# A pointwise convolution on TensorE: head and tail chunks side by side in one buffer, and a last supertile in two column parts

## The chip, the cores and the metric

One core of a Trainium2 chip. The metric is the device time of one execution in microseconds. The profiler's span is about 1.7 us shorter than the device time of the same execution (576.7 for 578.42 before the change).

## The reference, cut to what matters

```python
# x: (1, 384, 384, 384) bf16, dw: (1, 1, 384), pw: (384, 384)
out = x * dw[0, 0]                    # depthwise part with k = 1: a scale per channel
return einsum('bhwc,cd->bhwd', out, pw)
```

So it is one matrix product: 147,456 rows of 384 channels times a 384 x 384 matrix, whose rows are scaled by dw once at the start. 113 MB are read and 113 MB are written.

## The kernel before

The rows are cut into 288 supertiles of 512. VectorE transposes 32 x 32 blocks of a supertile's input (two instructions), TensorE makes 48 matmuls of 384 columns into four PSUM banks, ScalarE evicts the four banks (copies them out to SBUF) as bf16. Two PSUM sets alternate. Loads and stores move chunks of 1 to 10 supertiles, each chunk in the next of three input and three output buffers (an excerpt; comments are added):

```python
head, tail = [1, 1, 2, 2, 3, 4, 5], [7, 5, 4, 2, 1, 1]       # chunk sizes; 10 between
Xs = [bufp.tile([P, 4 * LMAX, C], BF16, name=f"X{i}") for i in range(NX)]      # NX = 3
Os = [bufp.tile([P, 4 * LMAX * D], BF16, name=f"O{i}") for i in range(NO)]     # NO = 3
...
with nc.tensor.Fori(0, NS // 2, 1) as it:                     # NS = 288
    rv = nc.tensor.to_reg(it + 1)
    for s in range(2):
        supertile(s, rv)                                      # 48 matmuls
...
for jj, (t, j) in enumerate(order):                           # evictions
    if j == 0 and t >= NO:
        nc.scalar.wait_ge(s_o[t % NO], 16 * (t // NO))        # store of chunk t - 3 has landed
    nq = 4
    if jj + 1 == NS:                                          # the last: VectorE takes half
        nq = 2
        ...
        e = nc.vector.tensor_copy(Ov[:, nq:4, j, :], PS[s][:, nq:4, :D])
    a = nc.scalar.copy(Ov[:, 0:nq, j, :], PS[s][:, 0:nq, :D])
```

The last supertile leaves in two stores, one issued by ScalarE (ACT in the profile) and one by the sync engine (SP), each of two 768-byte rows a partition.

## Time and profile before

| | before |
|---|---|
| device time, median of 3 (range) | 578.25 us (578.11 to 578.52) |
| span of the profiled execution | 576.7 us |
| TensorE busy | 98% |
| loop of matmuls, first to last | 7.40 to 571.22 us |
| TensorE's one pause | 19.31 to 21.11 us |
| last store issued, landed | 572.23, 575.3 us |

The lines behind these rows are in the prediction below.

### The profile page before, as it was taken

To read this page: it belongs to the slowest core of one execution; us is meant where nothing else is said; L and a number is where in the kernel's file an instruction comes from. 1 tells how busy PE (TensorE), PEld (TensorE's weight loads), DVE (VectorE), ACT (ScalarE), POOL (GpSimd) and SP (SyncE) were. 2 spreads that over 40 slices of the span, in tenths; PEclk is the share of its full clock that TensorE was granted. 3 is DMA by queue.
4 is the path that set the end of the run, shared out by engine and by line. 5 is a ranking of instruction groups with operands and counts; after the bars stand their busy time and mean duration, and the time that the engine had idled before them with its cause. 6 is when DMAs were issued, how large, how long until landed. Compare 5 with 4: busy or idle time off the path is not lost.

```text
span 576.7 us, 29717 instructions
## 1 busy us (share of the span) xinstructions
PE 567.1 (98%) x13871; PEld 356.0 (62%) x13871; DVE 508.8 (88%) x582; ACT 419.0 (73%) x296; POOL 1.7 (0%) x8
## 2 busy tenths in 40 slices
PE   8899999999999999999999999999999999999996
PEld 5566666666666666666666666666666666666663
DVE  6789999999999999999999999999999999999994
ACT  6677777777777777777777777777777777777774
POOL 1000000000000000000000000000000000000000
PEclk9999999999999999999999999999999999999999
DMA  7999999999999999999999999999999999986987
GB/s 243 388 432 436 422 424 425 432 439 421 407 388 438 386 392 395 430 398 384 404 421 400 394 405 425 387 386 427 405 386 394 427 407 389 400 356 272 365 342 266
DMA packets 25964, 226.88 MB, mean 393 GB/s; under 512 B 1249, under 2 KB 5218, under 8 KB 21986
## 3 DMA queue, kind: packets, MB, share of 16 engines
q1 hardware_dynamic: 25680, 226.60, 97.8%
q10 hardware_dynamic: 274, 0.20, 0.1%
q14 instruction: 9, 0.07, 0.0%
q8 instruction: 1, 0.02, 0.0%
HBM read 113.54 MB, written 113.25 MB: 393 GB/s over the span
## 4 chain that ended last, share of the span: by engine, by line
PE 96%; DMA 1%; ACT 1%; issue 0%; DVE 0%; POOL 0%; POOLq 0%; ACTq 0%; SPq 0%
PE ps L153 96%; DMA out_dram<-O 1%; ACT O L287 1%; PE ps L172 0%; ACT w_r L259 0%; DVE O L284 0%; PE ps L203 0%; POOL zero L220 0%; POOL warm L219 0%; POOLq L320 0%; PE ps L187 0%; ACTq L279 0%; SPq L93 0%
## 5 line engine op out<-in xcount | busy, mean ns | idle before, releaser
L153 PE MATMUL ps<-w_r,T 32*128 32x384 bf16 x13824 | 562.0, 321 | 2.7 <-ACT O L287 1.8
L246 DVE STREAM_TRANSPOSE T<-X 128x384 uint32<-128x384 uint32 x576 | 505.9, 881 | 56.4 <-DMA X<-in_x_dram 3.7
L287 ACT CAST O<-ps 128x1536 bf16<-128x1536 f32 x288 | 413.8, 1437 | 149.9 <-PE ps L153 147.1
L153 PEld LDWEIGHTS ps<-w_r,T 32*128 32x128 bf16 x13824 | 353.8, 93 | 210.8 <-ACT O L287 2.2
L259 ACT CAST w_r<-ps 128x768 bf16<-128x768 f32 x5 | 3.6, 818 | 1.6 <-PE ps L203 1.6
L172 PE MATMUL ps<-zero 32*128 32x384 bf16 x32 | 2.8, 516 | 1.4 <-POOL zero L220 1.4
L284 DVE CAST O<-ps 128x768 bf16<-128x768 f32 x1 | 1.0, 958 | 3.0 <-PE ps L153 3.0
L264 DVE COPY dw_f<-ps 128x3 f32<-128x3 f32 x1 | 0.2, 161 | 3.0 <-PE ps L187 3.0
L203 PE MATMUL ps<-pw_n,sel_w 128*128 128x384 bf16 x12 | 2.4, 329 | 0.0
L232 ACT ACT_TABLE_LOAD x1 | 1.3, 1283 | 1.5 <-SPq L93 1.5
L172 PEld LDWEIGHTS ps<-zero 32*128 32x128 bf16 x32 | 1.1, 118 | 2.0 <-issue 1.7
L203 PEld LDWEIGHTS ps<-pw_n,sel_w 128*128 128x128 bf16 x12 | 1.0, 99 | 1.7 <-DMA pw_n<-in_pw_dram 0.6
L259 DVE CAST w_r<-ps 128x768 bf16<-128x768 f32 x1 | 1.0, 958 | 0.9 <-PE ps L203 0.9
L268 DVE TENSOR_SCALAR sel_w<-sel,dw_f 128x512 bf16<-128x512 bf16 x3 | 0.9, 348 | 0.1
L222 POOL TENSOR_SCALAR_AFFINE_SELECT sel<-ones 128x512 bf16<-128x512 bf16 x1 | 0.7, 737 | 0.1
L221 POOL MEMSET ones<- 128x512 bf16 x1 | 0.5, 531 | 0.0
L187 PEld LDWEIGHTS ps<-ones,dw_row 1*128 1x128 bf16 x3 | 0.3, 127 | 0.3 <-issue 0.2
L232 ACT COPY warm<-warm 128x1 f32<-128x1 f32 x2 | 0.3, 188 | 0.0
L220 POOL MEMSET zero<- 128x192 uint32 x1 | 0.3, 258 | 0.0
L187 PE MATMUL ps<-ones,dw_row 1*128 1x1 bf16 x3 | 0.3, 174 | 0.0
L219 POOL MEMSET warm<- 128x3 f32 x1 | 0.1, 101 | 0.5 <-SPq L93 0.5
L309 POOL MEMSET const-bfloat16-1.0<- 128x1 bf16 x1 | 0.1, 102 | 0.0
(3 smaller groups left out, 0.3 us busy)
## 6 DMA issues: line engine op xcount, KB each, us to landing
X<-in_x_dram SPq DMA_DIRECT2D x25, 3840.0 KB, 21.9
out_dram<-O SPq DMA_DIRECT2D x25, 3840.0 KB, 27.9
X<-in_x_dram SPq DMA_DIRECT2D x2, 1920.0 KB, 14.6
out_dram<-O SPq DMA_DIRECT2D x2, 1920.0 KB, 16.8
X<-in_x_dram SPq DMA_DIRECT2D x2, 1536.0 KB, 10.4
out_dram<-O SPq DMA_DIRECT2D x2, 1536.0 KB, 13.5
X<-in_x_dram SPq DMA_DIRECT2D x1, 2688.0 KB, 20.1
out_dram<-O SPq DMA_DIRECT2D x1, 2688.0 KB, 12.0
```

The costliest lines, as they stand in the source:

```text
L153: mm = nc.tensor.matmul(PS[s][:, q, :D], lhsT=Ts[s][32 * q : 32 * q + 32, b, par::2], rhs=w_r[32 * q : 32 * q + 32, b, par, :], start=(b = ...
L172: nc.tensor.matmul(PS[0][:, i % 4, :D], lhsT=zero[32 * (i % 4) : 32 * (i % 4) + 32, 0:P], rhs=zero[32 * (i % 4) : 32 * (i % 4) + 32, :], s ...
L187: mm = nc.tensor.matmul(PS[1][:, k, D : D + 1], lhsT=dw_row[:, P * k : P * k + P], rhs=ones[0:1, 0, 0:1], start=True, stop=True,)
L203: mm = nc.tensor.matmul(w_ps(b)[:, r, :], lhsT=sel_w[:, b // 2, 2 * (b % 2) + r, :], rhs=pw_n[:, b // 2, :], start=True, stop=True,)
L221: nc.gpsimd.memset(ones[:], 1.0).then_inc(s_seed)
L222: nc.gpsimd.affine_select(out=sel[:].rearrange("p (v r) (q w) -> p v r q w", v=2, q=4), in_=ones[:].rearrange("p (v r) (q w) -> p v r q w" ...
L232: c = nc.scalar.copy(warm[:, s + 1 : s + 2], warm[:, 0:1])
L246: ins = nc.vector.transpose(out=Tw[:, 3 * h : 3 * h + 3], in_=Xw[:, :, j, 96 * h : 96 * h + 96].rearrange("p k (b w) -> p b k w", w=32),)
L259: i = nc.vector.tensor_copy(out, in_) if e == 0 else nc.scalar.copy(out, in_)
L268: nc.vector.tensor_scalar_mul(sel_w[:, k], sel[:], dw_f[:, k : k + 1]).then_inc(s_sw)
L284: e = nc.vector.tensor_copy(Ov[:, nq:4, j, :], PS[s][:, nq:4, :D])
L287: a = nc.scalar.copy(Ov[:, 0:nq, j, :], PS[s][:, 0:nq, :D])
```

## The change

Its intent is to take away the pause and to shorten the end. Chunks become groups: the small chunks of the head share one buffer, and so do those of the tail, so that none waits for another's store. At the end, the last supertile is computed in two column parts, so that what is evicted after the last matmul is smaller; for that the last four supertiles leave the loop. A new order of rows in the last load makes the last store one run of 3072 bytes a partition. The diff is an excerpt, with lines joined and comments added.

```diff
-    head, tail = [1, 1, 2, 2, 3, 4, 5], [7, 5, 4, 2, 1, 1]
+    head, tail = [[1, 1, 2, 2, 4]], [[6, 4], [3, 2, 1, 1, 1]]     # groups: one buffer each
...
-            if t >= NX: d._wait_ge(s_t[je % 2][1], je // 2 + 1)
+            if i == 0 and g >= NR:                                 # only a group's first chunk waits
+                nc.sync.wait_ge(s_t[je % 2][1], je // 2 + 1)
...
+            # last load:  xf[512 * first :, :].rearrange("(a k q) c -> q a k c", k=4, q=4)
+            # last store: of[512 * first :, :].rearrange("(m q) d -> m (q d)", q=4)
...
-        with nc.tensor.Fori(0, NS // 2, 1) as it:
+        with nc.tensor.Fori(0, NS // 2 - 2, 1) as it:
...
+        supertile(0, NS // 2 - 1)
+        supertile(1, NS // 2 - 1)
+        supertile(0, NS // 2)
+        for ps, c0, c1 in ((1, 0, DS), (0, DS, D)):                # DS = 256
+            ...                                                    # 48 matmuls of c1 - c0 columns
...
+                parts = [(s, 0, D, 2, 2 * jj + 2)]                 # supertile 286: both engines
+                parts = [(1, 0, DS, 2, 2 * jj + 1), (0, DS, D, 2, 2 * jj + 2)]   # the last
```

More of the change, by code (lines that the diff above doesn't have):

```diff
@@ L13, with _groups @@
 LMAX = 10
-NX = 3
-NO = 3
-def _chunks(n_super: int):
-    head, tail = [1, 1, 2, 2, 3, 4, 5], [7, 5, 4, 2, 1, 1]
-    mid = n_super - sum(head) - sum(tail)
+NR = 3
+DS = 256
+def _groups(n_super: int):
+    head, tail = [[1, 1, 2, 2, 4]], [[6, 4], [3, 2, 1, 1, 1]]
+    mid = n_super - sum(map(sum, head + tail))
     assert mid > 0 and mid % LMAX == 0
-    return head + [LMAX] * (mid // LMAX) + tail
+    return head + [[LMAX]] * (mid // LMAX) + tail
 @with_exitstack
@@ L51 @@
     NS = N // 512
-    chunks = _chunks(NS)
+    groups = _groups(NS)
+    chunks, first = [], 0
+    for g, ls in enumerate(groups):
+        for i, L in enumerate(ls):
+            chunks.append((g, i, sum(ls[:i]), first, L))
+            first += L
     NT = len(chunks)
-    s0 = [sum(chunks[:t]) for t in range(NT)]
+    g_end = [max(c[3] + c[4] for c in chunks if c[0] == g) - 1 for g in range(len(groups))]
     consts = ctx.enter_context(tc.tile_pool(name="consts", bufs=1))
@@ L68 @@
     zero = consts.tile([P, D], BF16, name="zero")
-    Xs = [bufp.tile([P, 4 * LMAX, C], BF16, name=f"X{i}") for i in range(NX)]
+    Xs = [bufp.tile([P, 4 * LMAX, C], BF16, name=f"X{i}") for i in range(NR)]
     Ts = [bufp.tile([P, NB, 256], BF16, name=f"T{i}") for i in range(2)]
-    Os = [bufp.tile([P, 4 * LMAX * D], BF16, name=f"O{i}") for i in range(NO)]
+    Os = [bufp.tile([P, 4 * LMAX * D], BF16, name=f"O{i}") for i in range(NR)]
     PS = [psum.tile([P, 4, 512], F32, name=f"ps{s}") for s in range(2)]
-    s_x = [nc.alloc_semaphore(f"s_x{i}") for i in range(NX)]
+    s_x = [[nc.alloc_semaphore(f"s_x{i}{k}") for k in range(max(map(len, groups[i::NR])))] for i in range(NR)]
     s_t = [[nc.alloc_semaphore(f"s_t{i}{h}") for h in range(2)] for i in range(2)]
@@ L79 @@
     s_d = nc.alloc_semaphore("s_d")
-    s_o = [nc.alloc_semaphore(f"s_o{i}") for i in range(NO)]
+    s_o = [nc.alloc_semaphore(f"s_o{i}") for i in range(NR)]
     s_dw = nc.alloc_semaphore("s_dw")
@@ L90 @@
     s_zero = nc.alloc_semaphore("s_zero")
-    s_last = nc.alloc_semaphore("s_last")
     with tc.tile_critical():
         def load_x(t):
-            L = chunks[t]
-            r = 512 * s0[t]
-            src = xf[r : r + 512 * L, :].rearrange("(p s) c -> p (s c)", p=P)
-            d = nc.sync.dma_start(Xs[t % NX][:, : 4 * L, :].rearrange("p s c -> p (s c)"), src)
-            if t >= NX:
-                je = s0[t - NX] + chunks[t - NX] - 1
-                d._wait_ge(s_t[je % 2][1], je // 2 + 1)
-            d.then_inc(s_x[t % NX], 16)
-        def store(t):
-            L = chunks[t]
-            r = 512 * s0[t]
-            je = s0[t] + L - 1
-            dst = of[r : r + 512 * L, :].rearrange("(q p j) d -> p q (j d)", q=4, p=P)
-            src = Os[t % NO][:, : 4 * L * D].rearrange("p (q e) -> p q e", q=4)
-            nc.sync.wait_ge(s_a[je % 2], je // 2 + 2)
-            nc.sync.dma_start(dst, src).then_inc(s_o[t % NO], 16)
+            g, i, off, first, L = chunks[t]
@@ new lines, in load_x @@
+            dst = Xs[g % NR][:, 4 * off : 4 * (off + L), :]
+            if t + 1 < NT:
+                src = xf[512 * first : 512 * (first + L), :].rearrange("(p s) c -> p (s c)", p=P)
+                dst = dst.rearrange("p s c -> p (s c)")
+            else:
+                src = xf[512 * first :, :].rearrange("(a k q) c -> q a k c", k=4, q=4)
+            if i == 0 and g >= NR:
+                je = g_end[g - NR]
+                nc.sync.wait_ge(s_t[je % 2][1], je // 2 + 1)
+            nc.sync.dma_start(dst, src).then_inc(s_x[g % NR][i], 16)
@@ new lines, in store @@
+        def store(t):
+            g, i, off, first, L = chunks[t]
+            je = first + L - 1
+            src = Os[g % NR][:, 4 * off * D : 4 * (off + L) * D]
+            if t + 1 < NT:
+                dst = of[512 * first : 512 * (first + L), :].rearrange("(q p j) d -> p q (j d)", q=4, p=P)
+                src = src.rearrange("p (q e) -> p q e", q=4)
+                nc.sync.wait_ge(s_a[je % 2], je // 2 + 2)
+                if je >= NS - 2:
+                    nc.sync.wait_ge(s_d, 1)
+            else:
+                dst = of[512 * first :, :].rearrange("(m q) d -> m (q d)", q=4)
+                nc.sync.wait_ge(s_a[1], NS // 2 + 2)
+                nc.sync.wait_ge(s_d, 3)
+            nc.sync.dma_start(dst, src).then_inc(s_o[g % NR], 16)
@@ L114 @@
         nc.scalar.dma_start(dw_row[:], dw.rearrange("a e c -> a (e c)")).then_inc(s_dw, 16)
         nc.sync.dma_start(pw_n[:], pw.rearrange("(k p) d -> p k d", p=P)).then_inc(s_pw, 16)
-        for t in range(NX + 1):
-            load_x(t)
-        for t in range(NT - 1):
-            for u in (t + NX, t + NX + 1):
-                if NX < u < NT and (u == t + NX) != (chunks[u - NX] == 1 and u - NX < 4):
-                    load_x(u)
-            store(t)
-        o_last = Os[(NT - 1) % NO][:, : 4 * D].rearrange("p (q e) -> p q e", q=4)
@@ L125 @@
-        of_last = of[N - 512 :, :].rearrange("(q p) d -> p q d", p=P)
-        nc.sync.dma_start(of_last[:, 2:4], o_last[:, 2:4])._wait_ge(s_d, 1).then_inc(
-            s_last, 16
-        )
-        for o in range(NO):
-            nc.sync.wait_ge(s_o[o], 16 * len(range(o, NT - 1, NO)))
-        nc.sync.wait_ge(s_last, 32)
+        todo = []
+        for t, (g, i, off, first, L) in enumerate(chunks):
+            todo.append((g_end[g - NR] if g >= NR else -1, load_x, t))
+            todo.append((first + L + 1, store, t))
@@ L137 @@
+        for _, f, t in sorted(todo, key=lambda a: a[0]):
+            f(t)
+        for o in range(NR):
+            nc.sync.wait_ge(s_o[o], 16 * sum(map(len, groups[o::NR])))
         w_eng = [1, 0, 1, 1, 1, 1]
@@ L216 @@
                 supertile(s, rv)
+        supertile(0, NS // 2 - 1)
+        supertile(1, NS // 2 - 1)
+        supertile(0, NS // 2)
+        for ps, c0, c1 in ((1, 0, DS), (0, DS, D)):
+            for b in range(NB):
+                for par in range(2):
+                    for q in range(4):
+                        if par == 0 and q == 0:
+                            if ps == 1 and b in (0, 3):
+                                nc.tensor.wait_ge(s_t[1][b // 3], NS // 2)
+                            if b == 0:
+                                nc.tensor.wait_ge(s_a[ps], NS // 2 + (ps == 0))
+                                if ps == 0:
+                                    nc.tensor.wait_ge(s_d, 1)
+                        mm = nc.tensor.matmul(
+                            PS[ps][:, q, : c1 - c0],
+                            lhsT=Ts[1][32 * q : 32 * q + 32, b, par::2],
+                            rhs=w_r[32 * q : 32 * q + 32, b, par, c0:c1],
+                            start=(b == 0 and par == 0),
+                            stop=(b == NB - 1 and par == 1),
+                            tile_position=(32 * q, 0),
+                        )
+            mm.then_inc(s_pe)
         nc.gpsimd.memset(warm[:], 0.0).then_inc(s_seed)
@@ L237, in transposes @@
         def transposes(t, j):
-            jj = s0[t] + j
-            L = chunks[t]
+            g, i, off, first, L = chunks[t]
+            jj = first + j
             s = jj % 2
-            Xw = Xs[t % NX][:].bitcast(U32)[:, : 4 * L, :].rearrange("p (k l) c -> p k l c", l=L)
+            Xw = Xs[g % NR][:].bitcast(U32)[:, 4 * off : 4 * (off + L), :].rearrange("p (k l) c -> p k l c", l=L)
             Tw = Ts[s][:].bitcast(U32).rearrange("p b (i k) -> p b k i", k=4)
@@ L244, in transposes @@
                 if h == 0 and j == 0:
-                    nc.vector.wait_ge(s_x[t % NX], 16 * (t // NX + 1))
+                    nc.vector.wait_ge(s_x[g % NR][i], 16 * sum(len(ls) > i for ls in groups[g % NR : g + 1 : NR]))
                 ins = nc.vector.transpose(
@@ L252, in transposes @@
                 ins.then_inc(s_t[s][h])
-        order = [(t, j) for t in range(NT) for j in range(chunks[t])]
+        order = [(t, j) for t in range(NT) for j in range(chunks[t][4])]
         def w_out(b):
@@ L274 @@
         for jj, (t, j) in enumerate(order):
-            L = chunks[t]
+            g, i, off, first, L = chunks[t]
             s = jj % 2
-            Ov = Os[t % NO][:, : 4 * L * D].rearrange("p (q j d) -> p q j d", q=4, d=D)
-            if j == 0 and t >= NO:
-                nc.scalar.wait_ge(s_o[t % NO], 16 * (t // NO))
-            nq = 4
-            if jj + 1 == NS:
-                nq = 2
-                nc.vector.wait_ge(s_o[t % NO], 16 * (t // NO))
-                e = nc.vector.tensor_copy(Ov[:, nq:4, j, :], PS[s][:, nq:4, :D])
-                e._wait_ge(s_pe, 2 * jj + 2)
-                e.then_inc(s_d)
-            a = nc.scalar.copy(Ov[:, 0:nq, j, :], PS[s][:, 0:nq, :D])
-            a._wait_ge(s_pe, 2 * jj + 2)
-            a.then_inc(s_a[s])
+            Ov = Os[g % NR][:, 4 * off * D : 4 * (off + L) * D].rearrange("p (q j d) -> p q j d", q=4, d=D)
+            if j == 0 and i == 0 and g >= NR:
+                nc.scalar.wait_ge(s_o[g % NR], 16 * sum(map(len, groups[g % NR : g : NR])))
+            if jj + 2 < NS:
+                parts = [(s, 0, D, 4, 2 * jj + 2)]
+            elif jj + 2 == NS:
+                nc.vector.wait_ge(s_o[g % NR], 16 * sum(map(len, groups[g % NR : g : NR])))
+                parts = [(s, 0, D, 2, 2 * jj + 2)]
+            else:
+                parts = [(1, 0, DS, 2, 2 * jj + 1), (0, DS, D, 2, 2 * jj + 2)]
+            for ps, c0, c1, nq, v in parts:
+                if nq < 4:
+                    e = nc.vector.tensor_copy(Ov[:, nq:4, j, c0:c1], PS[ps][:, nq:4, : c1 - c0])
+                    e._wait_ge(s_pe, v)
+                    e.then_inc(s_d)
+                a = nc.scalar.copy(Ov[:, 0:nq, j, c0:c1], PS[ps][:, 0:nq, : c1 - c0])
+                a._wait_ge(s_pe, v)
+                a.then_inc(s_a[s])
             if jj + 2 < NS:
                 transposes(*order[jj + 2])
-        nc.scalar.dma_start(of_last[:, 0:2], o_last[:, 0:2])._wait_ge(s_a[(NS - 1) % 2], (NS - 1) // 2 + 2).then_inc(
-            s_last, 16
-        )
 _INS = ['x', 'dw', 'pw']
```

## The prediction

> **What bounds the kernel now.** I read the busy table first, then the chain of waits, then the head and the tail in order of time. A "supertile" below is 512 rows of x: 48 matmuls into four PSUM banks, one eviction, two vector transposes.
>
> ```profile
> PE 567.1 (98%) x13871; PEld 356.0 (62%) x13871; DVE 508.8 (88%) x582; ACT 419.0 (73%) x296; POOL 1.7 (0%) x8
> ...
> L153 PE MATMUL ps<-w_r,T 32*128 32x384 bf16 x13824 | 562.0, 321 | 2.7 <-ACT O L287 1.8
> L246 DVE STREAM_TRANSPOSE T<-X 128x384 uint32<-128x384 uint32 x576 | 505.9, 881 | 56.4 <-DMA X<-in_x_dram 3.7
> L287 ACT CAST O<-ps 128x1536 bf16<-128x1536 f32 x288 | 413.8, 1437 | 149.9 <-PE ps L153 147.1
> ```
>
> TensorE works 98% of the span, so only its edges can move: before its first matmul, its one pause, and after its last. The chain in order of time shows all three.
>
> ```profile
> 7.40 2.16 PE ps L153 x48
> 9.56 0.02 issue
> 9.58 1.45 ACT O L287
> 11.03 0.02 issue
> 11.05 8.49 DMA out_dram<-O
> 19.54 0.02 issue
> 19.56 0.02 ACTq L279
> 19.57 0.04 issue
> 19.62 1.45 ACT O L287
> 21.07 0.05 issue
> 21.11 550.11 PE ps L153 x13536
> 571.22 0.02 issue
> 571.25 0.96 DVE O L284
> ```
>
> Matmuls begin at 7.40. The first supertile takes 2.16 us; from 21.11 on, 282 supertiles take 550.11 us without a break, 1.951 us each. The pause lies between: supertiles 1 to 5 end at 9.56 + 5 x 1.951 = 19.31, the next starts at 21.11, so TensorE loses 1.80 us. The chain names the reason: the fourth chunk wants output buffer 0 again, and the first chunk's store, issued at 11.05, lands only 8.49 us later. ScalarE then evicts late, and the matmuls wait for their banks. The stretch view confirms that the pause is whole, and shows the tail.
>
> ```profile
> 19.30:21.10 1.80, 0.00 (x0) 0.00 (x0) 1.80 (x4) 1.48 (x2) 0.00 (x0) 1.00 0.94 378
> ...
> 571.30:572.20 0.90, 0.00 (x0) 0.00 (x0) 0.90 (x1) 0.74 (x1) 0.00 (x0) 1.00 1.04 348
> 572.20:574.20 2.00, 0.00 (x0) 0.00 (x0) 0.00 (x1) 0.00 (x0) 0.00 (x0) 1.00 1.02 317
> ```
> ```profile
> 571.24 0.80 ACT L287 CAST O<-ps 128x768 bf16<-128x768 f32 x1 [0.51 <-PE ps L153]
> 571.25 0.96 DVE L284 CAST O<-ps 128x768 bf16<-128x768 f32 x1 [3.02 <-PE ps L153]
> 572.07 0.50 ACTq L292 DMA_DIRECT2D out_dram<-O  x1
> 572.23 0.37 SPq L126 DMA_DIRECT2D out_dram<-O  x1
> ```
>
> After the last matmul (571.22) come a halved eviction (0.96 us, the VectorE half is the longer), the issue of two 192 KB stores, 3.1 us to landing (the DMA view's figure for the later one), so 572.23 + 3.1 = 575.3, and 1.4 us to the end of the span at 576.7. In these last microseconds the DMA engines are still full (shares 1.04 and 1.02), so earlier stores are draining beside the final one.
>
> **What the Trainium skill says.** "TensorE: Matmul & The Clock Gate", section "Back-to-back issue gap", gives a warm matmul N/2.4 + 2.5 ns for N columns. Four row groups run at once here, so 384 columns should cost (160 + 2.5)/4 = 40.6 ns; the trace has 550.11/13536 = 40.64. It agrees, and I use it for the narrower matmuls. The same page, section "Wait — 56ns, not 53.3ns?", puts a floor of about 25 ns between the starts of matmuls however narrow; no row of this trace tests it, though the weight loads last 93 ns, and 93/4 = 23 ns points to the same place. "DMA: Bandwidth & Descriptors", section "Anatomy of one DMA — SWDGE (gpsimd) path", fits about 2.0 us + bytes/436e3; for 393 KB that is an estimate of 2.9 us (its fit is for the other issue path; the trace's 288 KB weight load took 2.9 and its first 384 KB load 3.4). "Runtime: NRT & Kernel Launch", section "Instruction fetch mechanics", gives TensorE room for 2048 instructions; it bears on the first rival.
>
> **The change part by part.**
>
> 1. Shared buffers at the head. Chunks 1, 1, 2, 2, 4 now lie side by side in buffer 0, and the next two groups of 10 have buffers of their own. No output buffer is reused before supertile 30, which starts near 9.56 + 29 x 1.951 = 66 us. I estimate when the group's last store lands: the 30 supertiles of loads (11.8 MB) are queued first and at the 400 GB/s of the long stretch end near 33 us; six supertiles of stores, the fourth group's load and the last store of group 0 follow and end near 53 us. So that wait has over 12 us to spare and the pause goes: -1.80 us. The loads must not bring a new one. With pw (0.29 MB) ahead and 0.393 MB a supertile from 2.3 us, the chunks land near 5, 6, 8, 10 and 14 us and the ten of group 1 near 24 us; the vector engine needs that group at about 25 us and can lose 1 us more. Tight, but I count 0. The start at 7.40 is set by the weights (ScalarE's three copies of w_r), which the change leaves alone.
>
> 2. The loop. TensorE makes 142 passes over a pair of supertiles instead of 144, then runs three whole supertiles written out, with the same instructions in the same order, and the split last one: 0.
>
> 3. The last supertile in two column parts. 48 matmuls of 256 columns: (106.7 + 2.5)/4 = 27.3 ns, 1.31 us. 48 of 128 columns: the formula gives 14 ns, but the floor and the weight loads, which are as many as before, say 25: 1.20 us. Together 2.51 against 1.95: +0.56 us. The second part needs the four banks of supertile 286, now evicted by both engines in 0.96 us, done about 1.05 us after its last matmul; the first part lasts 1.31, so no gap.
>
> 4. The last eviction. It shrinks from 768 to 256 elements a partition. VectorE: 958 ns for 768 and 161 ns for the 3-element copy give 1.04 ns an element, so 161 + 256 x 1.04 = 428 ns: -0.53 us. The first part's half (about 0.69 us for 512) is done inside the 1.20 us of the second.
>
> 5. The last store. One 384 KB store from the sync queue with 3072 contiguous bytes a partition in place of two of 192 KB with 768-byte rows. Same bytes on the same 16 engines. The supertiles before it are stored in smaller pieces (3, 2, 1, 1) and 286 leaves about 0.5 us sooner, so less should be draining beside it: I take 3.0 for 3.1, -0.1 us.
>
> 6. The last load takes 768-byte rows, so that the four output rows of a partition are neighbours. It is requested long before its use: 0.
>
> Sum: -1.80 + 0.56 - 0.53 - 0.1 = -1.87 us. 578.25 - 1.87 = 576.4 us. In the trace: last matmul near 571.22 - 1.80 + 0.56 = 569.98, store issued near 570.5, landed near 573.5, span near 574.8.
>
> **The rivals.** First, an instruction stall: code that followed no loop is now fetched while DMA is nearly full (97.8% for the main queue). For it: over 240 matmuls written out. Against: with their weight loads they and the loop make some 700 instructions, below the 2048 named. If it came, one to three microseconds between supertiles 283 and 287, and 577.5 to 579. Second, DMA as the bound: the main queue is 97.8% busy, and if the 11.8 MB of head loads ran at 300 GB/s like the mixed traffic at 7.40 to 19.30 (295), group 1 would land near 31 us and TensorE would wait some 4 us, a new pause in place of the old: 580. Against: that stretch had engines idle for want of issued loads (share 0.91), while 3 to 5 us ran near 400. A weaker form has the backlog reach the last store: +0.5 to 1 us. Third, the narrow part may stream at 14 ns (its formula without the floor): then VectorE's first-part eviction comes in the way a little and 0.5 us more is gained: 575.9. Or each matmul with its weight load costs 40 ns whatever its width: two parts of 1.95, 1.4 us worse than my sum, 577.8, which eats most of the gain.
>
> **Range and chances.** The pause is the surest term (1.80, nearly whole); parts 3 to 5 sum to about 0 with an uncertainty near 0.8 us; the old runs spread over 0.4 us. That gives 576.4, range 575.2 to 578.0. Two per cent is 11.6 us: to gain it one would have to remove most of what is not matmul (578.25 - 562.0 = 16 us), and to lose it DMA would have to starve TensorE for many microseconds. Faster 0.01, within 2% 0.98, slower 0.01.
>
> **What would show it.** Right: one unbroken run of matmuls from 7.4 to about 570; no wait of ScalarE for a store near 19 us; 48 narrow-part matmuls in about 1.2 us and 48 middle ones in 1.3; a last VectorE eviction near 0.43 us; a last store that lands in about 3 us. Wrong: VectorE waiting for x near 25 us with TensorE idle after it; TensorE idle after 560 without a releaser; two parts near 1.95 us each; or a last store well over 3.1 us.

## The result, and the profile after

Measured: 577.18 us (577.07 to 577.50, 4 runs) against 578.18 for the kernel before (577.51 to 578.52, 4 runs). The ratio is 0.9985, with a 95% interval of 0.9968 to 1.0002. A ratio here and below is not quite the ratio of the medians. It is about 1.0 us faster by the medians, and the interval just includes no change at all.

First the group of TensorE's whole supertiles on the page of the changed kernel, and, from its groups kept apart by shape, the last eviction (line, engine, operation, output and input, count, then busy time and mean ns of one, then idle time before it).

```profile
L162 PE MATMUL ps<-w_r,T 32*128 32x384 bf16 x13776 | 559.8, 321 | 0.9 <-ACT w_r L292 0.9
```
```profile
L322 DVE CAST O<-ps 128x256 bf16<-128x256 f32 x1 | 0.4, 423 | 0.0
```

The wait of 1.8 us for ScalarE is gone from the matmuls' idle column, and the last eviction took 423 ns, where the prediction worked out 428. Now its chain in order of time (start, duration, what):

```profile
7.67 559.83 PE ps L162 x13776
567.51 1.33 PE ps L241 x48
...
568.86 0.69 DVE O L322
...
569.56 0.42 DVE O L322
```

One unbroken run of matmuls from 7.67: the pause has gone, and no store is in the chain. The 256-column part took 1.33 us. The 128-column part is not in the chain because it was over (569.51) before VectorE was free from the first part's eviction. It took 0.67 us for 48 matmuls, 14 ns each.

What did not go as hoped is the very end. The DMA issues after 570 us (KB, us from issue to landing), then stretches of half a microsecond after it (last two columns: mean busy share of the 16 DMA engines, and GB/s):

```profile
out_dram<-O SPq DMA_DIRECT2D x1, 384.0 KB, 3.9
```
```profile
572.00:572.50 0.50, 0.00 (x0) 0.00 (x0) 0.00 (x0) 0.00 (x0) 0.00 (x0) 1.00 0.17 61
572.50:573.00 0.50, 0.00 (x0) 0.00 (x0) 0.00 (x0) 0.00 (x0) 0.00 (x0) 1.00 0.13 52
573.00:573.50 0.50, 0.00 (x0) 0.00 (x0) 0.00 (x0) 0.00 (x0) 0.00 (x0) 1.00 0.09 37
```

A share of 0.13 is two engines of sixteen. By the trace's packet records at least twelve engines had written their last semaphore (the mark that an engine has finished its share) by 572.06 and all but two by 572.6; these two ended at 573.26 and 573.54. So the store took 3.9 us, not 3.1. The accounts of the two profiled executions, in us:

| part | before | after | difference |
|---|---|---|---|
| start of the loop | 7.40 | 7.67 | +0.27 |
| loop start to end of supertile 286 | 561.87 | 559.84 | -2.03 |
| last supertile | 1.95 | 2.00 | +0.05 |
| last matmul to issue of the last store | 1.01 | 0.57 | -0.44 |
| issue to landing | 3.1 | 3.9 | +0.8 |
| landing to the end of the span | 1.37 | 1.32 | -0.05 |
| sum = span | 576.7 | 575.3 | -1.4 |

Two questions remain: why two engines are late, and why the times (1.0 us apart, later less) gain less than the traces (1.4 us).

### The profile page after: what moved, and what is told of

Its sections match the earlier page's. It is cut to its first block, busy times and chain, and to the rows that moved or that the text cites. A ratio compares the mean times of both kernels' runs of the same rounds, so it can differ in the third digit from the quotient of the medians.

```text
span 575.3 us, 29802 instructions
## 1 busy us (share of the span) xinstructions
PE 567.2 (99%) x13919; PEld 415.8 (72%) x13919; DVE 509.9 (89%) x584; ACT 418.2 (73%) x297; POOL 1.7 (0%) x8
## 4 chain that ended last, share of the span: by engine, by line
PE 98%; ACT 0%; DVE 0%; issue 0%; POOL 0%; POOLq 0%; SPq 0%
PE ps L162 97%; PE ps L181 0%; ACT w_r L292 0%; PE ps L241 0%; DVE O L322 0%; PE ps L212 0%; POOL zero L253 0%; POOL warm L252 0%; POOLq L355 0%; PE ps L196 0%; SPq L99 0%
## 5 line engine op out<-in xcount | busy, mean ns | idle before, releaser
L162 PEld LDWEIGHTS ps<-w_r,T 32*128 32x128 bf16 x13776 | 411.6, 93 | 149.1 <-issue 1.2
L322 DVE CAST O<-ps 128x768 bf16<-128x768 f32 (+2 forms) x3 | 2.1, 691 | 1.4 <-PE ps L162 1.1
L241 PE MATMUL ps<-w_r,T 32*128 32x256 bf16 (+1 forms) x96 | 2.2, 241 | 0.0
L241 PEld LDWEIGHTS ps<-w_r,T 32*128 32x128 bf16 x96 | 2.0, 93 | 0.2
```

What stands on the lines that cost most here:

```text
L162: mm = nc.tensor.matmul(PS[s][:, q, :D], lhsT=Ts[s][32 * q : 32 * q + 32, b, par::2], rhs=w_r[32 * q : 32 * q + 32, b, par, :], start=(b = ...
L241: mm = nc.tensor.matmul(PS[ps][:, q, : c1 - c0], lhsT=Ts[1][32 * q : 32 * q + 32, b, par::2], rhs=w_r[32 * q : 32 * q + 32, b, par, c0:c1] ...
L322: e = nc.vector.tensor_copy(Ov[:, nq:4, j, c0:c1], PS[ps][:, nq:4, : c1 - c0])
```

## The experiments

Theory F: the code that now stands outside the loop makes TensorE's sequencer fetch more pages of instructions, each on one DMA engine, which is then late with its share of the last store. What started it is this line of the DMA queues, first of the kernel before, then of the changed one (packets, MB, share):

```profile
q8 instruction: 1, 0.02, 0.0%
```
```profile
q8 instruction: 3, 0.05, 0.0%
```

By the packet records of the trace these are packets of 16,384 bytes; the changed kernel's two new ones began at 565.47 and 569.86 us and took 0.96 and 1.34 us. Theory S: the single store is slow of itself. Kernels of one group of four ran on one chip and shared the runs of the kernel before.

**1. The changed kernel again** (no edit).

> The changed kernel as it is, so that the others are compared on the same chip. Reference for two theories of why its last store took 3.9 us to land and not 3.0. Theory F: TensorE's written-out code makes its sequencer fetch 16 KB pages of instructions at about 565.5 and 569.9 us; each goes through one DMA engine, which then finishes its share of the last store late. Theory S: the single store with one 3072-byte run a partition is slow of itself. Both expect here: span 575.3 +- 0.3, three 16 KB instruction packets, last store landing in 3.9 us.

Measured: 577.49 us median against 577.53 before, ratio 0.9993 (0.9980 to 1.0006). Span 576.0, three packets again, one engine done only at 574.23, so that the store landed in 4.2 us, later than the 3.9 expected. The loop began at 8.06 us, 0.39 later than in the first profile. The gain was smaller than in the first comparison; the start differs between executions of one kernel, which run 7 takes up.

**2. Head alone**: groups and buffers of the change, with loop, last eviction, last load and two last stores as before.

```diff
-        with nc.tensor.Fori(0, NS // 2 - 2, 1) as it:     # and what follows it
+        with nc.tensor.Fori(0, NS // 2, 1) as it:
-            nc.sync.dma_start(dst, src)                   # one last store
+            nc.sync.dma_start(of_last[:, 2:4], o_last[:, 2:4]) ; nc.scalar.dma_start(of_last[:, 0:2], o_last[:, 0:2])
```

> Shared buffers and chunk sizes of the change alone: loop, last eviction, last load and the two last stores as before the change. Both theories: the pause near 19 us is gone (2.0 us with the restart), one 16 KB instruction packet only, last stores landing in about 3.1 us: span 574.7, that is 2.0 us under the kernel before and 0.6 us under the changed kernel. If the head instead hides some cost in the middle, the span is nearer 576.

Measured: 577.03 us median, ratio 0.9991 (0.9978 to 1.0004), level with the changed kernel. Span 575.1 with a start at 8.06, so 567.1 from loop start to the end, against 567.6 and 567.9 for the changed kernel. One instruction packet. By this comparison the pause is what the change gains; its tail as a whole gave nothing on top.

**3. Tail alone**: chunks and buffers of the kernel before, with the written-out supertiles, the split and the single store.

```diff
+                nc.vector.wait_ge(s_o[(t + 1) % NO], 16 * ((t + 1) // NO))   # buffer of the last chunk
+                parts = [(s, 0, D, 2, 2 * jj + 2)]                            # ahead of supertile 286's half
```

> Written-out supertiles, split last one and single store alone, with the chunks and buffers of the kernel before. Both theories: pause kept, last VectorE eviction about 0.5 us earlier after the last matmul, last store landing in about 3.9 us; span 577.0 to 577.1, no faster than the kernel before. If the tail's own gain counted (the prediction's sum without the pause), 576.6.

Measured: 582.0 us median, ratio 1.0075 (1.0060 to 1.0089): 4.5 us slower, a miss, and partly of my making. With separate buffers the last chunk's output buffer must be free first, and I had VectorE wait for that before its half of supertile 286. From its chain:

```profile
564.69 8.30 DMA out_dram<-O
573.11 0.97 DVE O L321
```

VectorE stands until an earlier store has landed, and the second part of the last supertile, which needs the banks of supertile 286, stands with it. So this run does not price the tail alone. It does show that an early end needs the tail's buffers side by side.

**4. Six supertiles written out** in place of four.

```diff
-        with nc.tensor.Fori(0, NS // 2 - 2, 1) as it:
+        with nc.tensor.Fori(0, NS // 2 - 3, 1) as it:     # one more pair after it
```

> The changed kernel with six supertiles written out and not four, so that the instruction pages are crossed at other places: by my count near 561.5 and 566.5 us, the second over 3 us before the last store is issued. Theory F: last store lands in 3.0 to 3.3 us and the span falls to 574.5 to 574.7. Theory S: landing 3.9 us and span 575.3 as before.

Measured: 576.89 us median, ratio 0.9987 (0.9974 to 1.0000). The packets moved as counted, to 561.21 and 567.38 us. The last store landed in 3.4 us: better than 3.9, not the 3.0 to 3.3 expected. Two engines were still late, by about 0.6 and 1.1 us. Towards F, but not decisive.

**5. Head chunks in separate buffers**, all else as changed.

```diff
-    head, tail = [[1, 1, 2, 2, 4]], [[6, 4], [3, 2, 1, 1, 1]]
+    head, tail = [[1], [1], [2], [2], [4]], [[6, 4], [3, 2, 1, 1, 1]]
```

> The changed kernel, but its five head chunks each in a buffer of their own in turn, so that the fourth chunk again waits for the first one's store. If that wait is the pause, TensorE restarts near 20.9 to 21.1 us whenever it began, and the span is the changed kernel's plus 2.0 us less what a late start already took: 576.5 to 577.5. If the pause in the kernel before came from the small loads and not from the output buffer, the same, but the chain names the load and not the store.

Measured: 580.91 us median, ratio 1.0053 (1.0039 to 1.0066), 3 us above the kernel before and more than expected. Its waits (engine and tile, for what, total, times, longest):

```profile
ACT O L325 <- DMA out_dram<-O: 2.0, 1, 2.0
PE ps L162 <- DVE T L279: 1.7, 1, 1.7
```

ScalarE's wait for the first store is back, and TensorE pauses 1.06 us and restarts at 21.05. But there is a second pause of 1.7 us, until 30.73: the first load of ten supertiles was issued only at 14.14 and took 15.5 us. Its input buffer was free at 13.12, when the last transpose out of it ended; the load then stood behind a store on the sync queue, which waited for its own eviction and was issued at 13.70. Sharing therefore saves two waits. The kernel before shows no second pause; that its graded chunks of 3, 4 and 5 are the reason was not tried.

**6. Single store in the loop**: the head-alone kernel with the one-run store and the last load that goes with it.

```diff
-            nc.sync.dma_start(of_last[:, 2:4], o_last[:, 2:4]) ; nc.scalar.dma_start(of_last[:, 0:2], o_last[:, 0:2])
+            nc.sync.dma_start(of_last, o_last)            # (m q) d -> m (q d): 3072 bytes a partition
```

> The head-only kernel (loop not written out, one page of instructions only) with the changed kernel's one-run single store and its last load. Theory F (pages of instructions): the last semaphore writes come 2.5 to 2.8 us after the last store is issued, as with head only. Theory S (the single store is slow): 3.3 us or more.

Measured: 575.98 us median against 577.83 before, ratio 0.9969 (0.9956 to 0.9983): the fastest so far. All sixteen engines wrote their last semaphore by 573.16, 1.97 us after the issue, within 0.15 us of each other; both theories had expected more, 2.5 us at the least. The issues at the end of the head-alone kernel (two stores), and of this one:

```profile
out_dram<-O ACTq DMA_DIRECT2D x1, 192.0 KB, 2.5
out_dram<-O SPq DMA_DIRECT2D x1, 192.0 KB, 2.9
```
```profile
out_dram<-O SPq DMA_DIRECT2D x1, 384.0 KB, 2.3
```

Theory S falls: the single store is the quicker form, 2.3 us against 2.9. What makes it 3.9 in the changed kernel would then come with the written-out code or with the split.

**7. The kernel before with a late start, and 8. the head-alone kernel with the same.**

```diff
+        idle_work(2)                                      # 16 matmuls on zeros
         with nc.tensor.Fori(0, NS // 2, 1) as it:
```

> The kernel before with 16 idle matmuls (0.65 us) ahead of the loop. If the pause ends when the first store lands, at about 19.5 us, whatever the start, a later start is swallowed by a shorter pause: restart still at 20.9 to 21.1 us, and the time within 0.2 us of the kernel before. If the pause is a fixed cost, +0.65 us.

> The head-only kernel with the same 16 idle matmuls ahead of the loop. It has no pause that could swallow them: 0.65 us more than the head-only kernel had against the kernel before (ratio 0.9991), so about equal to or 0.2 us over the kernel before. If both late kernels lose the same, the pause does not absorb the start.

Measured: 578.38 us median, ratio 1.0004 (0.9990 to 1.0017), for the kernel before; 577.78, ratio 1.0003 (0.9989 to 1.0017), for head alone. The first lost 0.0004 by it, the second 0.0012 (from 0.9991, on another chip). That is the order expected, but the intervals overlap, so the times alone don't decide. The traces do. The chain of the delayed kernel before:

```profile
8.42 2.16 PE ps L153 x48
...
12.06 7.02 DMA out_dram<-O
...
20.66 542.31 PE ps L153 x13344
```

The loop began 1.02 us later than in the first profile (8.42 for 7.40), and the matmuls restarted 0.45 us earlier (20.66 for 21.11; 20.9 to 21.1 was expected). The store that ends the pause landed at 19.1 and 19.5 us in the two, and did not follow the start. The pause itself shrank from 1.80 to 20.66 - (8.42 + 2.16 + 5 x 1.951) = 0.33 us. Run 3 shows the same without any delay put in: its loop began at 8.28, restarted at 20.89, and the pause was 0.70 us. So the pause takes up a late start, and a kernel without it does not.

One more number of run 8 bears on the end of the kernel: its later last store landed in 3.5 us, against 2.9 for the same end in run 2, with two engines done at 573.71 and 574.07 and the others by 573.12. It has neither written-out code nor a split.

And the start is late by chance. The twelve matmuls that prepare the weights, in the kernel before and in the single-store kernel of run 6:

```profile
L203 PE MATMUL ps<-pw_n,sel_w 128*128 128x384 bf16 x12 | 2.4, 329 | 0.0
```
```profile
L215 PE MATMUL ps<-pw_n,sel_w 128*128 128x384 bf16 x12 | 3.0, 421 | 0.0
```

The same instructions took 2.4 to 3.7 us in the fourteen profiles, and undelayed loops began between 7.40 and 8.30 us. The Trainium skill, "TensorE: Matmul & The Clock Gate", section "Part 1: The HAM clock gate", says that the array runs at half clock until a busy window of about 3.4 us has passed, and that the window runs free of the kernel. The traces agree: the record of full clock begins anywhere from 4.19 to 7.42 us (at the earliest 2.8 us after the first matmul at 1.43, so less than a whole window of matmuls was enough), and where it begins before 4.3 the undelayed loop starts at 7.40 or 7.42, after 6 us at 8.28 or 8.30. The stretch recorded at full clock has one of two lengths in all fourteen traces, 566.61 or 570.03 us, and these differ by 3.41 us.

**9. Single store, four whole supertiles written out**: run 6 with only that.

```diff
-        with nc.tensor.Fori(0, NS // 2, 1) as it:
+        with nc.tensor.Fori(0, NS // 2 - 2, 1) as it:     # then four whole supertiles
```

> The kernel of the loop with the single store, with nothing changed but that its last four supertiles (whole, not split) are written out. Theory F: two more 16 KB instruction packets near 565 and 570 us, and the last semaphore writes 3.2 to 3.8 us after the last store is issued in place of 1.97, one or two engines far behind the others; the time 1.2 to 1.8 us above the single store in the loop. Theory S or any other (the store's shape): landing 2.0 us and the same time.

Measured: 576.08 us median against 577.88, ratio 0.9973 (0.9959 to 0.9986): not slower, a miss for theory F as I had put it. The trace shows why. This code is 48 matmuls shorter than the changed kernel's, so one more page was fetched, not two, and it came at 565.19 us. Its queue and its last store:

```profile
q8 instruction: 2, 0.03, 0.0%
```
```profile
out_dram<-O SPq DMA_DIRECT2D x1, 384.0 KB, 2.6
```

With the 768 KB store that follows that page, fourteen engines wrote their last semaphore by 568.10 us and two at 568.87 and 568.95. One late engine is there without any page too (in run 6 the others by 569.00, one at 569.22, and with the store ahead of that the others by 565.92, one at 567.08); the second I put down to the page. Both caught up in the idle DMA time before the later stores, where on average nine of the sixteen engines stood idle between 569.0 and 569.5, and in the last store one engine is 0.2 us late. By this reading, which rests on one profile, a page costs little if the engine has time to catch up.

**10. Single store in the loop again, and 11. the changed kernel a third time**, side by side.

> The single store in the loop again, beside the changed kernel on one chip: it should again be some 0.3% under the kernel before, and 1.0 to 1.5 us under the changed kernel, with all last semaphore writes within 0.1 us of each other.

> The changed kernel a third time, for that comparison: 0.05 to 0.15% under the kernel before; span less start of the loop 567.5 to 568.0 us; one or two engines late with the last store.

Measured, on one chip: 576.32 us median (ratio 0.9977, 0.9964 to 0.9991) and 577.40 (0.9989, 0.9976 to 1.0003). The gain of the single store in the loop holds, a little smaller than 0.3%. From loop start to the end of the span the two took 566.5 and 567.5 us. The end of run 10, to be held against the stretches of the changed kernel above:

```profile
572.00:572.50 0.50, 0.00 (x0) 0.00 (x0) 0.00 (x0) 0.00 (x0) 0.00 (x0) 0.80 1.02 406
572.50:573.00 0.50, 0.00 (x0) 0.00 (x0) 0.00 (x0) 0.00 (x0) 0.00 (x0) 0.50 0.56 215
```

All engines stop together; there is no thin end.

**12. Two supertiles written out, page borders moved.**

```diff
-            with nc.tensor.Fori(0, n, 1) as _:            # warm-up: a loop of 8 matmuls, 384 columns
+            for i in range(18 * n):                       # 36 written out, 160 columns
-        with nc.tensor.Fori(0, NS // 2 - 2, 1) as it:
+        with nc.tensor.Fori(0, NS // 2 - 1, 1) as it:
```

> The changed kernel with two supertiles written out, and the warm-up matmuls written out too (36 of 160 columns in place of 16 of 384, twice), which moves page borders by some 56 matmuls. Theory F: one page is fetched near 566 to 567 us, where the DMA engines still have some idle time, and none at the end: last semaphore writes 2.0 to 2.6 us after issue, and span less start of the loop about 566.1 to 566.6 us, level with or 0.4 under the single store in the loop. If written-out code costs in another way, 567.5 as in the changed kernel.

Measured: 576.81 us median, ratio 0.9985 (0.9972 to 0.9999); loop start to end 567.4 us, not the 566.1 to 566.6 hoped for. One page, at 565.99 for 1.11 us, none at the end; still the last store landed in 3.6 us. Two engines were late, by 1.1 us with the store after the page, by 1.0 and 1.2 with the next, and by 0.5 and 1.2 in the last, while thirteen were done by 571.8. With the split the last three stores are issued closer together (566.79, 568.34 and 569.80 us here; 566.81, 568.76 and 570.30 in run 9), so an engine that is behind finds less idle time to catch up. With a page at nearly the same place the last engine ended 0.2 us after the others without the split (run 9) and 1.2 us with it. But the engine that is behind in every kernel came to these last stores with different arrears: in the store of three supertiles before them it was 1.7 us behind in run 9 and 2.2 here.

The runs by the form of their end, without run 3, which had a wait of its own, and the kernel before (microseconds; the landing is that of the DMA view, the later of two where there are two; the last column is where an 8,192-byte packet of another instruction queue, q14, began, counted from the issue of the last store):

| kernel | 16 KB pages after 560 us | last matmuls split | loop start to issue of last store | landing | q14 packet |
|---|---|---|---|---|---|
| single store in the loop (6, 10) | none | no | 562.9 | 2.3, 2.3 | -0.8, -0.8 |
| single store, written out (9) | 565.2 | no | 562.9 | 2.6 | -0.3 |
| two stores in the loop (2, 8) | none | no | 562.8 | 2.9, 3.5 | -0.1, +0.5 |
| six written out (4) | 561.2, 567.4 | yes | 562.4 | 3.4 | +0.1 |
| two written out (12) | 566.0 | yes | 562.4 | 3.6 | +0.7 |
| separate head buffers (5) | 569.0, 573.3 | yes | (pauses) | 4.1 | +0.0 |
| as changed (first profile, 1, 11) | two each, 565.5 to 566.1 and 569.9 to 571.4 | yes | 562.4 | 3.9, 4.2, 3.8 | +0.7, +0.1, +0.2 |

The split saves 0.5 us up to the issue of the last store, and late engines take back 1.1 to 1.9 us of landing, measured against the single store in the loop.

Theory F in its first form, pages alone, falls with run 9. The reading that fits best is that engines behind their fellows, some of them behind a page, have no idle time left to catch up in once the end is compressed by the split. It is not the only one: run 8 landed late with neither.

One engine's arrears can be followed through the whole kernel. Each engine writes a semaphore when its share of a transfer has landed, so the sixteenth write of a transfer tells how far the last engine is behind. It came 0.1 us after the fifteenth at 72 us, 5.5 at 221 and 8.6 at 507 in the changed kernel (0.05, 3.8 and 6.1 in run 10), and 7.6 to 10.4 us at the worst in all fourteen traces. As the stores become small this shrinks, to 1.3 to 2.2 us in the store before the last four in the runs with the shared tail, run 8 apart, which had 2.7. That it is always the same engine is inferred from the steady growth.

**What stays open.** That the pages are TensorE's is inferred: their number follows only what is written out after the loop (one packet in every kernel with the whole loop, two or three otherwise). That the split with no page at all in the last ten microseconds would land in 2.3 us was not tried; all four split arrangements (as changed, 4, 5 and 12) fetched a page there. Nor was the q14 packet of the table varied on its own. It takes 0.31 us, so that it can be a part of the lateness only; but where it began before the last store was issued, the store landed in 2.3 to 2.9 us, and where it began after, in 3.4 to 4.2 us. Run 3 is the exception (3.7 us), with the q14 packet 4.4 us before its last store and a 16 KB page that began with it. The kernel before fits in too (0.04 us before and 3.1 us in the first profile, 0.2 us after and 3.5 us in run 7). The records do not name the DMA engine of a packet, so that the page's engine is one of the late ones is inferred from the order in time and from sizes (a second late engine appears in the first store after the page, 0.8 to 1.1 us behind after pages of 0.96 and 1.11 us). Why one engine falls behind in every kernel, with or without pages, is not known. So the shares of page, split, arrears and q14 packet in the lateness are not told apart. Shown is that every arrangement with split and pages landed late, and that neither the single store in the loop nor one page without the split did.

## Why the prediction was right or wrong, point by point

The time of 577.18 us lies inside the range of 575.2 to 578.0, and "within 2%" was right. The difference of 1.0 us is about half of the 1.87 predicted, and in the two later comparisons (runs 1 and 11) the ratios of 0.9993 and 0.9989 come to 0.4 and 0.6 us. That the total is not further off is partly luck: part 3 was 0.5 us too dear and part 5 0.9 us too cheap.

- Part 1, the pause: right, and a little larger in the profile compared (2.03, not 1.80). Counted from start to start, the seventh supertile should have begun at 7.40 + 6 x 1.950 = 19.10 and began at 21.11, so 2.01 us were lost; a count from the end of a supertile leaves out 0.2 us in which the last matmuls before the pause run out. What the step missed is that 1.80 was one execution's value. It shrinks when the loop starts late (0.70 us in run 3, 0.33 us in run 7), so the average gain is smaller. The start itself, which the sum took as fixed at 7.40, came at 7.67, 8.06 and 8.28 in the three profiles of the changed kernel.
- The tight count of the head loads held: TensorE had no wait after 7.67 us in the profile, and the first load of ten supertiles landed at 24.3 us, for 24 counted.
- Part 3, +0.56 us for the split: wrong in size; +0.05 was measured. The failing term is the 25 ns assumed for a 128-column matmul with its weight load. It took 14 ns, which is the width formula without the floor, as in the third rival. That rival's 0.5 us arrived at the last store's issue, and was lost in its landing.
- Part 4, the last eviction: right, 423 ns for 428. Of the 0.53 us saved 0.44 arrived at the store's issue, because VectorE came from the first part's eviction only at 569.55 and the issue followed 0.1 us after the copy.
- Part 5, -0.1 us for the last store: this is the step that failed. The one-run store by itself is better than the step said (2.3 us, for 2.9 and 3.5 with two stores in runs 2 and 8). In the changed kernel it took 3.9 us, +0.8 (4.2 and 3.8 in runs 1 and 11), because two engines were behind: the step counted bytes for the sixteen engines together, where the slowest one decides. Why they were behind stays open, as said above.
- The first rival named the fetching of instructions but looked for the harm on TensorE, as a stall between supertiles. Fetches came, and TensorE never waited for them; if they did harm, it was to the DMA engines in the last microseconds. The weaker form of the second rival, a backlog that costs the last store 0.5 to 1 us, is nearest to what was seen, only that it sat in two engines and not in all.

A better kernel came out of the experiments: groups and shared buffers of the change, the whole loop, the last eviction halved as before, and the single store. It was 0.23% and 0.31% under the kernel before in two comparisons (both with intervals clear of 1; run 9, written out, is level with it at 0.27%), and beside the changed kernel on one chip 576.32 against 577.40 us.

## What to carry to other kernels

Small chunks at the head belong side by side in one buffer: a rotation of buffers makes the fourth small chunk wait for the first one's store. Near the end of a kernel the DMA engines are part of the critical path one by one: a store ends when its slowest engine ends, so look at how many engines are busy in the last stretches, and count instruction pages as transfers, too. And a pause whose end does not follow the start hides jitter ahead of it; to price it, look at more than one execution.

## What the Trainium skill lacked or had wrong

- "TensorE: Matmul & The Clock Gate": the floor of about 25 ns between matmul starts did not hold for 32-row matmuls in four row groups, each with its own weight load: 48 of 128 columns took 0.67 us, 14 ns each, so the width formula applied unaltered. "Part 3" of the same page has about 4 ns between the starts of matmuls in different row groups; the section with the floor doesn't say that the floor leaves these out.
- "Runtime: NRT & Kernel Launch": it gives TensorE room for 2048 instructions and calls the cost of a page border mostly hidden. For TensorE that held: it never waited, though two more 16,384-byte packets appeared with 240 matmuls written out, in a program that the prediction put at some 700 TensorE instructions. What the page lacks is the cost on the DMA side: each packet took 0.96 to 1.34 us of the DMA queue in the first profile.
- "DMA: Bandwidth & Descriptors": the fit of 2.0 us + bytes/436e3, 2.9 us for 393 KB, is stated for the other issue path; the store from the SP queue with 3072 bytes a partition landed in 2.3 us at best and in 4.2 at worst.
- No page gives an amount by which one DMA engine trails the others in a long stream: here the sixteenth semaphore write of a transfer came after the fifteenth by 7.6 to 10.4 us at the worst, by kernel, with all transfers issued from the sync and scalar queues.
